# Norms of a segment made together, ahead of the first stacks, and the second weight group fetched behind x

## The chip, the cores and the metric

The kernel runs on one core of a Trainium2 chip. The core has TensorE (PE in the profile; PEld is its weight load) for matmuls, VectorE (DVE), ScalarE (ACT), GpSimd (POOL), and SyncE (SP), on whose queue this kernel issues its DMAs. Each engine works through its own list of instructions in order; semaphores make one engine wait for another. The metric is device time in microseconds (us), less is better.

## The reference

One block of a transformer whose layer norms are modulated by a condition vector c. First a memory-augmented causal attention over four segments of 512 tokens (32 heads of 32), then a mixer MLP across the tokens. Cut to what matters:

```python
mod = silu(c) @ w_mod                       # six rows of 1024: sa, ca, ga, sb, cb, gb
h = layernorm(x) * (1 + ca) + sa            # x: 2048 x 1024, float32
q, k, v = h @ wq, h @ wk, h @ wv            # 32 heads
for s in range(4):                          # segments of 512 tokens
    p = softmax(q[s] @ k[s].T * scale + mask)
    o[s] = g * (phi(q[s]) @ M) / (phi(q[s]) @ z) + (1 - g) * (p @ v[s])
    M += phi(k[s]).T @ v[s];  z += phi(k[s]).sum()
x = x + ga * (o @ wo)
h = layernorm(x) * (1 + cb) + sb
x = x + gb * (w2.T @ gelu(w1.T @ layernorm(h) + b1) + b2)     # over the tokens
```

Only the first two lines and the beginning of the third and fourth, the opening of the kernel, are touched by the change.

## The kernel before, in words

All large products keep close to float32 accuracy by splitting each operand into a rounded high part and the rest (`split`: a cast for the high part, a subtraction for the low part) and making three matmuls of the parts.

*First segment.* SP fetches, in this order: half of the weights for the scale row 1 + ca (`wms`), the four x tiles of segment 0 (128 tokens by 1024), the other half, then eight tiles `wm` for the shift sa, with the first group's attention weights (`rawv`, `rawq`) between them, then the four x tiles of segment 1. TensorE makes the scale row in two halves (`scale_row`, L273); VectorE copies each half out of PSUM (`scale_columns`, L279), and small matmuls (L281) turn it into columns. Meanwhile `norm_x` normalises each x tile by itself: statistics on VectorE (L130, L132), Ln and Exp on ScalarE (L133, L134), four small VectorE operations (L136 to L138, L218), and a pass over the tile on ScalarE (L219). Then come eight chunks of 128 channels: `h_chunk` transposes the four tiles' columns on TensorE (L224), ScalarE applies scale and shift (L226), and a split makes a page (a tile `h`, 128 channels by 512 tokens, high and low part; 16 buffers, so both segments' 8 pages have room). `first_chunk` multiplies each page with the weights as soon as it is there: keys and values (`nps`, L195) and queries (`qps`, L203). VectorE also makes one pass over a `wm` tile per chunk (L314) for the shift.

*Steps.* Attention then goes by steps t: t = 0 is weight group 0 (four heads) with segment 0, t = 1 the same group with segment 1, t = 2 and 3 are group 1 with segments 0 and 1, and so on. `project(t, piece)` has four pieces: two halves of keys and values with their copies out of PSUM (L380, L381, L386), then the transposes of the keys (`kps`, L395) with the queries, their split into `sg`, and the stacks of heads 0 to 2 (three small DMAs each, L356 to L358, `sk` from `sg`), then the stack of head 3 and the memory update (L445). For t = 0 the matmuls are `first_chunk`'s. The maxima (L463), scores (L499 and following) and values (L528) of a head come in the loop behind.

*Weights.* Six float32 tiles of a group are made by `split_part` from three raw fetches (`raw`: 3 buffers), into `w`, which has 8 buffers. `keep_w` writes the six to DRAM (`wsp`, L176) so that the second pass over the groups reads them back. Before the change the second group is fetched by `load_w(1, 0)` from the loop, behind the last stack of step 0 on SP's queue.

*Order.* The program text gives every instruction a priority, earlier text first; `tc.high_priority()` puts a block ahead. The order of each engine's list is then worked out when the kernel is built, by a planner that runs the program against a modelled clock (`schedule_with_timeline_sim=True`) and takes, on each engine, the ready instruction of highest priority. `tc.issue_after(i)` ties what is traced in its block to come behind instruction i, on the engine of i only. So a change of one place can move the order elsewhere.

Of the kernel before, what the change touches and what calls it, by code (L numbers as in the profile page):

```python
# [7 lines left out]
F32 = mybir.dt.float32  # L8
# [3 lines left out]
AF = mybir.ActivationFunctionType  # L12
ALU = mybir.AluOpType
# [5 lines left out]
P = 128  # L19
# [6 lines left out]
EPS = 1e-5  # L26
# [18 lines left out]
def attention_and_mlp(ctx, tc, x, wq, wkv, wo, beta, w1, b1, w2, b2, c, wm_a, wm_b, out):  # L45
    nc = tc.nc
    V, A, G, T, SY = nc.vector, nc.scalar, nc.gpsimd, nc.tensor, nc.sync
# [13 lines left out]
    const = ctx.enter_context(tc.tile_pool(name="const", bufs=1))  # L61
# [3 lines left out]
    a = par.__enter__()  # L65
    scb, gaw = (a.tile([P, D], F32, name=n) for n in ("scb", "gaw"))
    acst_pool = tc.tile_pool(name="acst", bufs=1)
    acst = acst_pool.__enter__()
# [6 lines left out]
    def bank(tag, bufs, name):  # L75
        return psum.tile([P, 512], F32, tag=tag, bufs=bufs, name=name)

    A.preload_act_table_set("natural_log_exp_and_others")
    ident = top.tile([P, P], F32, name="ident")
# [14 lines left out]
    eps = const.tile([P, 1], F32, name="eps")  # L94
# [17 lines left out]
    saca = acst.tile([P, NK, 2], F32, name="saca")  # L112
# [5 lines left out]
    def split(dst, src, hi_eng, lo_eng):  # L118

        hi, lo = dst[:, 0], dst[:, 1]  # L120
        if hi_eng is A:
            last_hi[0] = A.copy(hi, src)  # L122
        else:
            hi_eng.tensor_copy(hi, src)
        lo_eng.tensor_tensor(lo, src, hi.bitcast(F32), op=ALU.subtract)  # L125

    def ln_stats(pool, src, tag):
        st = const.tile([P, 2, 6], F32, tag="st", bufs=4, name="st")
        for i in range(2):
            V.bn_stats(st[:, i], src[:, 512 * i:512 * i + 512])  # L130
        mv = const.tile([P, 4], F32, tag="mv", bufs=4, name="mv")
        V.bn_aggr(mv[:, 0:2], st)  # L132
        A.activation(mv[:, 2:3], mv[:, 1:2], AF.Ln, bias=eps)  # L133
        A.activation(mv[:, 2:3], mv[:, 2:3], AF.Exp, scale=-0.5)  # L134
        v, r0, t = mv[:, 1:2], mv[:, 2:3], mv[:, 3:4]
        V.tensor_scalar(t, v, EPS, r0, op0=ALU.add, op1=ALU.mult)  # L136
        V.tensor_scalar(t, t, -0.5, r0, op0=ALU.mult, op1=ALU.mult)
        V.tensor_scalar(r0, t, 1.5, r0, op0=ALU.add, op1=ALU.mult)  # L138
        return mv
# [4 lines left out]
    def new_page(name):  # L144
        return page.tile([P, 2, 512], F32R, tag="page", bufs=16, name=name)
# [5 lines left out]
    def fetch_part(g, kind, part):  # L151
        r = a.tile([P, D], F32, tag="raw", bufs=3, name=f"raw{kind}{g}_{part}")
        SY.dma_start(r, (wkv if kind == "v" else wq)[g, :, 1024 * part:1024 * part + 1024])
        return r

    def split_part(g, kind, part, r):

        for i in range(2):
            w = aw.tile([P, 2, 512], F32R, tag="w", bufs=8, name=f"w{kind}0_{g}_{part}_{i}")
            split(w, r[:, 512 * i:512 * i + 512], A, V)  # L160
            W[0, g][kind, 2 * part + i] = w
# [11 lines left out]
    def keep_w(g):  # L173
        for kind, n in (("v", 4), ("q", 2)):
            for i in range(n):
                SY.dma_start(wsp[g, i if kind == "v" else 4 + i], W[0, g][kind, i].bitcast(F32))  # L176
# [8 lines left out]
    W = {}  # L185
# [25 lines left out]
        SY.dma_start(t, x[P * tt:P * tt + P])  # L211
        return t

    last_norm = [None]

    def norm_x(pool, t):
        mv = ln_stats(pool, t, "a")
        last_norm[0] = V.tensor_scalar(mv[:, 3:4], mv[:, 0:1], -1.0, mv[:, 2:3], op0=ALU.mult, op1=ALU.mult)  # L218
        A.activation(t, t, AF.Identity, scale=mv[:, 2:3], bias=mv[:, 3:4])  # L219

    def h_chunk(pool, xs, seg, ct):
        ps = bank(*(("s1", 2), ("s2", 2))[ct % 2] if seg else ("s2", 2), f"hps{seg}_{ct}")
        for i in range(4):
            T.transpose(ps[:, 128 * i:128 * i + 128], xs[i][:, P * ct:P * ct + P], ident)  # L224
        h32 = pool.tile([P, L], F32, tag="h32", bufs=HB, name=f"h32_{seg}_{ct}")
        A.activation(h32, ps, AF.Identity, scale=saca[:, ct, 1:2], bias=saca[:, ct, 0:1])  # L226
        pg = new_page(f"h{seg}_{ct}")
        split(pg, h32, V if seg else A, V if ct % 2 or not seg else G)
        hpages[seg, ct] = pg

    def token_tile(tt):

# [21 lines left out]
    s2p = right.__enter__()  # L254
    left = tc.tile_pool(name="st1", bufs=1)
    s1p = left.__enter__()
# [9 lines left out]
    bc = s1p.tile([P, NK, P], F32, name="bc")  # L266
    rows = MZ.rearrange("p g n -> p (g n)")[0:1]

    def scale_row(cb):
        ps = bank(*(("ms", 1), ("s1", 2))[cb], f"srow{cb}")  # L270
        with tc.high_priority():
            for k in range(NK):
                mm = T.matmul(ps[0:1], sc[:, k:k + 1], scale_wm[4 * cb + k // 2][:, k % 2], start=(k == 0),  # L273
                              stop=(k == NK - 1))
        return ps, mm

    def scale_columns(cb, ps):
        with tc.issue_after(last_norm[0].ins):
            V.tensor_copy(rows[:, 512 * cb:512 * cb + 512], ps[0:1])  # L279
        for ct in range(4 * cb, 4 * cb + 4):  # L280
            T.matmul(scale_ps[:, ct:ct + 1], rows[:, P * ct:P * ct + P], ident[0:1, 0:1], start=True, stop=True,  # L281
                     skip_group_check=True)
        V.tensor_scalar_add(saca[:, 4 * cb:4 * cb + 4, 1], scale_ps[:, 4 * cb:4 * cb + 4], 1.0)

    fetch_scale(0)
    xs = {0: [load_x(s1p, tt) for tt in range(4)]}
# [8 lines left out]
        q_chunk(W[0, 0], h, ct, first[2])  # L295

    srow = [scale_row(0)]
    with tc.high_priority():
        for t in xs[0]:
            norm_x(s1p, t)  # L300
    srow.append(scale_row(1))
    V.tensor_copy(bc, sc.unsqueeze(2).to_broadcast([P, NK, P]))
    for i in range(2):
        ps = bank("s2", 2, f"scps{i}")
        with tc.issue_after(srow[0][1].ins):
            for j in range(4):
                T.transpose(ps[:, 128 * j:128 * j + 128], bc[:, 4 * i + j], ident)
        A.copy(scb[:, 512 * i:512 * i + 512], ps)
    for cb in range(2):
        scale_columns(cb, srow[cb][0])  # L310
    for ct in range(NK):
# [14 lines left out]
    b = late.__enter__()  # L326
# [19 lines left out]
    st = {}  # L346

    last_sk = {}
# [232 lines left out]
    seg_x = {}  # L581

    def seg_load(seg):
        seg_x[seg] = [load_x(s2p, tt) for tt in range(4 * seg, 4 * seg + 4)]
        for t in seg_x[seg]:
            norm_x(s2p, t)

    def seg_chunks(seg, lo, hi):
        for ct in range(lo, hi):
            h_chunk(s2p, seg_x[seg], seg, ct)  # L590

    def spread(dst, i):
        SY.dma_start(dst, bass.AP(tensor=modd.tensor, offset=modd.offset + D * i, ap=[[0, P], [1, D]]))

    project(0, 0)
    project(0, 1)
    with tc.issue_after(last_wm.ins):
        seg_load(1)
    project(0, 2)
    project(0, 3)  # L600
    seg_chunks(1, 0, 8)
    project(1, 0)
    project(1, 1)
    project(1, 2)
    project(1, 3)
    with tc.issue_after(last_sk[0, 3].ins):
        keep_w(0)
    right.__exit__(None, None, None)
    right = tc.tile_pool(name="late2", bufs=1, side="right", reuse_waits="tile")
    r_ = right.__enter__()  # L610
# [47 lines left out]
    for n in range(-LEADS, 4 * NI + VL):  # L658
# [3 lines left out]
        m = n + LEADP  # L662
        if 0 <= m + 4 < 4 * NI:
            t = (m + 4) // 4
# [5 lines left out]
        if 59 <= m < 67:  # L670
            seg, ct = 2 + (m - 59) // 4, 2 * ((m - 59) % 4)
            reload_h(seg, ct)
            reload_h(seg, ct + 1)
        if 4 * NI - 5 <= m < 4 * NI + 3:
            i = m - 4 * NI + 5
# [434 lines left out]
```

## Time and profile before

| what | value |
|---|---|
| median of 3 runs | 2245.69 us (2245.46 to 2247.83) |
| the profiled execution's own time | 2248.87 us |
| its span | 2247.2 us |
| TensorE busy, share of the span | 2196.9 us, 98% |
| VectorE, ScalarE, GpSimd busy | 1670.9, 1144.3, 725.4 us |
| DMA, mean over the span | 188 GB/s |

A row of the timeline reads: start, time, engine, line, operation, output<-input, shape, count, and in brackets how long the engine had been idle before and what ended that. Rows of the same kind are merged, so a row can span a pause; matmul ends are modelled. A row of a table of stretches gives the busy time of each engine in a stretch. A row of the waits gives who waited for whom, the total, how many times, and the longest. The chain that ended last is the path back from the last instruction through whatever released each step.

### The profile page before, as it was taken

The numbers are of one execution on the slowest core, as the hardware profiler recorded it, in microseconds if no ns is written. First come the engines' busy times: TensorE is split into PE (matmuls) and PEld (weight loads), VectorE is DVE, ScalarE is ACT, GpSimd is POOL, SyncE is SP. The second block draws the span as 40 slices with busy tenths as digits, with TensorE's granted clock in tenths as the row PEclk, the third lists the DMA queues.
The fourth block names the chain that finished last, engine by engine and source line by source line (L and its number), as shares of the span: only waits on it lengthen the run. The fifth ranks groups of instructions, "written<-read, shape, count | busy, mean of one in ns | idle before, by whom it ended". The sixth has DMA issues, their size and how long they took to land.

```text
span 2247.2 us, 38334 instructions
## 1 busy us (share of the span) xinstructions
PE 2196.9 (98%) x13786; PEld 1890.3 (84%) x13786; DVE 1670.9 (74%) x3782; ACT 1144.3 (51%) x2098; POOL 725.4 (32%) x831
## 2 busy tenths in 40 slices
PE   8999999998999999999999999999999999999999
PEld 5889898887988899988888888888888888888887
DVE  6677677766677677665758866788888887868687
ACT  5477777665666666655546633533334242424232
POOL 1166666655766677655001200033330000000000
PEclk9999999999999999999999999999999999999999
DMA  7656565687567566674664587755556541414134
GB/s 267 199 169 186 162 190 165 181 290 228 145 188 223 164 185 196 192 215 161 225 217 154 215 323 272 262 188 221 206 202 239 204 155 57 155 57 145 57 122 150
DMA packets 175187, 423.06 MB, mean 188 GB/s; under 512 B 17525, under 2 KB 71829, under 8 KB 166037
## 3 DMA queue, kind: packets, MB, share of 16 engines
q1 hardware_dynamic: 174996, 420.61, 57.3%
q8 instruction: 110, 1.80, 0.3%
q14 instruction: 81, 0.66, 0.1%
HBM read 244.62 MB, written 125.06 MB: 165 GB/s over the span
## 4 chain that ended last, share of the span: by engine, by line
PE 85%; DMA 5%; DVE 4%; ACT 2%; POOL 2%; issue 1%; SPq 1%; DVEq 0%; ACTq 0%; POOLq 0%
PE mx L890 47%; PE nps L195 12%; PE qps L203 7%; PE po L760 6%; PE pv L528 3%; DMA sk<-sg 1%; PE sz L463 1%; PE a L499 1%; PE sx L463 1%; PE a L502 1%; PE sy L463 1%; POOL ph L514 1%; PE rd L435 1%; DMA sk<-nt 1%; PE up L445 1%
## 5 line engine op out<-in xcount | busy, mean ns | idle before, releaser
L890 PE MATMUL mx<-bU,sp 128*128 128x512 f32 x2352 | 534.2, 389 | 0.9 <-DVE ac L897 0.9
L890 PEld LDWEIGHTS mx<-bU,sp 128*128 128x128 f32 x2352 | 441.2, 188 | 93.4 <-issue 1.3
L195 PE MATMUL nps<-wv,h 128*128 128x256 f32 x3072 | 436.2, 282 | 0.0
L122 ACT CAST sp<-wr 128x384 fp32r<-128x384 f32 (+2 forms) x408 | 217.1, 545 | 425.0 <-PE mx L890 357.6
L890 PE MATMUL mx<-bA,sp 128*128 128x512 f32 x1764 | 430.5, 389 | 0.0
L514 POOL TENSOR_TENSOR ph<-p,ph 128x640 f16<-128x640 f32 x256 | 377.5, 1496 | 150.1 <-ACT ph L512 148.3
L195 PEld LDWEIGHTS nps<-wv,h 128*128 128x128 f32 x3072 | 405.0, 189 | 6.2
L890 PEld LDWEIGHTS mx<-bA,sp 128*128 128x128 f32 x1764 | 331.1, 188 | 68.8
L125 DVE TENSOR_TENSOR sp<-wr,sp 128x384 fp32r<-128x384 f32 (+2 forms) x408 | 259.4, 646 | 28.3 <-ACT sp L122 28.1
L897 DVE TENSOR_TENSOR ac<-mx,ac 128x512 f32<-128x512 f32 x280 | 189.1, 684 | 84.7 <-PE mx L890 84.1
L203 PE MATMUL qps<-h,wq 128*128 128x512 f32 x768 | 200.4, 404 | 0.0
L512 ACT CAST ph<-p 128x1280 f16<-128x1280 f32 x128 | 161.0, 1259 | 45.8 <-POOL p L510 45.2
L760 PE MATMUL po<-wo,ots 128*128 128x512 f32 x768 | 179.3, 390 | 0.0
L760 PEld LDWEIGHTS po<-wo,ots 128*128 128x128 f32 x768 | 143.5, 188 | 29.0
L203 PEld LDWEIGHTS qps<-h,wq 128*128 128x128 f32 x768 | 143.4, 193 | 28.0
L510 POOL TENSOR_SCALAR_AFFINE_SELECT p<-p 128x256 f32<-128x256 f32 x256 | 129.0, 513 | 109.1 <-ACT p L507 61.3
L890 PE MATMUL mx<-bB,sp 128*128 128x512 f32 x588 | 164.0, 389 | 0.0
L528 PE MATMUL pv<-vp,ph 128*128 128x97 bf16 (+1 forms) x2560 | 144.4, 203 | 2.4 <-POOL ph L514 1.6
L465 DVE CUSTOM_DVE_ANT_0 sx<-sx,mask 128x128 f32<-128x128 f32 (+1 forms) x256 | 93.7, 366 | 60.6 <-PE sx L463 58.5
L528 PEld LDWEIGHTS <-ph 128*128 128x128 f16 x2560 | 115.6, 99 | 24.9 <-issue 10.0
L890 PEld LDWEIGHTS mx<-bB,sp 128*128 128x128 f32 x588 | 110.3, 188 | 22.9
L897 DVE TENSOR_TENSOR cc<-mx,cc 128x512 f32<-128x512 f32 x140 | 94.7, 683 | 36.5 <-PE mx L890 36.4
(199 smaller groups left out, 3158.2 us busy)
## 6 DMA issues: line engine op xcount, KB each, us to landing
sk<-sg SPq DMA_DIRECT2D x384, 128.0 KB
wr<-in_w_dram SPq DMA_DIRECT2D x28, 1024.0 KB
wr<-in_w_dram SPq DMA_DIRECT2D x32, 768.0 KB
bstu<-ucd SPq DMA_DIRECT2D x28, 768.0 KB
wsp<-wv SPq DMA_DIRECT2D x32, 512.0 KB
rawm<-in_wm_b_dram SPq DMA_DIRECT2D x32, 512.0 KB
wv<-wsp SPq DMA_DIRECT2D x32, 512.0 KB
pcd<-cc SPq DMA_DIRECT2D x14, 1024.0 KB
```

The lines of the kernel that those rows point to most:

```text
L122: last_hi[0] = A.copy(hi, src)
L125: lo_eng.tensor_tensor(lo, src, hi.bitcast(F32), op=ALU.subtract)
L195: T.matmul(ps[:, aa], h[:, j, 128 * tt:128 * tt + 128], wt[:, i, o:o + 256], start=(n == 0), stop=(n >= 6 * NK - 2), skip_group_check=True)
L203: T.matmul(ps, wt[:, i, o:o + 128], h[:, j], start=(k + n == 0), stop=(3 * k + n == 3 * NK - 1))
L465: marks[4 * t + h - LEADS, "V"] = V.tensor_tensor_reduce(o, o, mask[:, 384 - 128 * i:], 1.0, -3.0e38, op0=ALU.add, op1=ALU.max, accum_out= ...
L510: G.affine_select(w, w, pattern=[[0, 2], [1, 128]], compare_op=ALU.is_ge, fill=0.0, base=0, channel_multiplier=-1)
L512: marks[n, "A"] = A.copy(ph[:, 0], p32)
L514: marks[n, "G"] = G.tensor_tensor(ph[:, 1, c], p32[:, c], ph[:, 0, c], op=ALU.subtract)
L528: T.matmul(pv[:, i, 0:w], ph[:, part, o:o + 128], d["vp"][:, j, h, 0:w], start=(n == 0), stop=(n == 19), skip_group_check=True)
L760: T.matmul(ps, os_[:, i, P * ct:P * ct + P], wop[ct, nh][:, j], start=(n == 0), stop=(n == 3 * NK - 1))
L890: T.matmul(ps, ops[q][:, i, P * k:P * k + P], b[:, j], start=(m == 0 and first), stop=(m == 3 * nk - 1), skip_group_check=True)
L897: V.tensor_tensor(d, ps, d, op=ALU.add)
```

## The change

- `norm_all` takes four tiles. VectorE makes all statistics into one tile `mv4`; one Ln and one Exp on 128x4, four small VectorE operations on 128x4 (now `scalar_tensor_tensor`), then the passes over the tiles: the first and third on ScalarE (`activation`), the second and fourth on VectorE (`tensor_scalar`). All of it has high priority. It returns marks: the last statistics, the Exp, and the last pass of either engine. `norm_x` stays for the tiles of segments 2 and 3.
- First segment: the transposes of sc and their copies (L307, L308) stand ahead of the norms and lose their tie to the first scale row. The copies of the scale rows are tied to the last statistics instead of the last norm.
- Second segment: `seg_load(1)` stands ahead of `project(0, 0)`. ScalarE's part of pieces 0 and 1 is tied behind its Exp; VectorE's part of everything down to piece 3 behind its last tile pass. The pages 0 and 1 of segment 1 come next, and pieces 2 and 3 of step 0, with the stacks, are tied behind ScalarE's and VectorE's work for page 1. The other six pages follow.
- Weights: the three raw fetches of group 1 are issued right behind x of segment 1; the splits are tied behind page 1 on both engines; `keep_w(1)` is tied behind the last stack of step 0, as `keep_w(0)` is. The loop finds group 1 present and does not load it.

No arithmetic of the result is left out.

```diff
--- before.py
+++ after.py
@@ -122,7 +122,7 @@
             last_hi[0] = A.copy(hi, src)
         else:
             hi_eng.tensor_copy(hi, src)
-        lo_eng.tensor_tensor(lo, src, hi.bitcast(F32), op=ALU.subtract)
+        return lo_eng.tensor_tensor(lo, src, hi.bitcast(F32), op=ALU.subtract)
 
     def ln_stats(pool, src, tag):
         st = const.tile([P, 2, 6], F32, tag="st", bufs=4, name="st")
@@ -211,11 +211,33 @@
         SY.dma_start(t, x[P * tt:P * tt + P])
         return t
 
-    last_norm = [None]
+    def norm_all(tiles):
+
+        with tc.high_priority():
+            m = acst.tile([P, 5, 4], F32, tag="mv4", bufs=1, name="mv4")
+            r, t, nb = m[:, 2], m[:, 3], m[:, 4]
+            mv = m[:, 0:2].rearrange("p a b -> p (a b)").rearrange("p (i a) -> p i a", a=2)
+            for k, src in enumerate(tiles):
+                st = const.tile([P, 2, 6], F32, tag="st", bufs=4, name="st")
+                for i in range(2):
+                    V.bn_stats(st[:, i], src[:, 512 * i:512 * i + 512])
+                last_stats = V.bn_aggr(mv[:, k], st)
+            A.activation(r, mv[:, :, 1], AF.Ln, bias=eps)
+            exp = A.activation(r, r, AF.Exp, scale=-0.5)
+            V.scalar_tensor_tensor(t, mv[:, :, 1], EPS, r, op0=ALU.add, op1=ALU.mult)
+            V.scalar_tensor_tensor(t, t, -0.5, r, op0=ALU.mult, op1=ALU.mult)
+            V.scalar_tensor_tensor(r, t, 1.5, r, op0=ALU.add, op1=ALU.mult)
+            V.scalar_tensor_tensor(nb, mv[:, :, 0], -1.0, r, op0=ALU.mult, op1=ALU.mult)
+            for k, src in enumerate(tiles):
+                if k % 2:
+                    last_v = V.tensor_scalar(src, src, r[:, k:k + 1], nb[:, k:k + 1], op0=ALU.mult, op1=ALU.add)
+                else:
+                    last_a = A.activation(src, src, AF.Identity, scale=r[:, k:k + 1], bias=nb[:, k:k + 1])
+        return last_stats, exp, last_a, last_v
 
     def norm_x(pool, t):
         mv = ln_stats(pool, t, "a")
-        last_norm[0] = V.tensor_scalar(mv[:, 3:4], mv[:, 0:1], -1.0, mv[:, 2:3], op0=ALU.mult, op1=ALU.mult)
+        V.tensor_scalar(mv[:, 3:4], mv[:, 0:1], -1.0, mv[:, 2:3], op0=ALU.mult, op1=ALU.mult)
         A.activation(t, t, AF.Identity, scale=mv[:, 2:3], bias=mv[:, 3:4])
 
     def h_chunk(pool, xs, seg, ct):
@@ -223,10 +245,11 @@
         for i in range(4):
             T.transpose(ps[:, 128 * i:128 * i + 128], xs[i][:, P * ct:P * ct + P], ident)
         h32 = pool.tile([P, L], F32, tag="h32", bufs=HB, name=f"h32_{seg}_{ct}")
-        A.activation(h32, ps, AF.Identity, scale=saca[:, ct, 1:2], bias=saca[:, ct, 0:1])
+        act = A.activation(h32, ps, AF.Identity, scale=saca[:, ct, 1:2], bias=saca[:, ct, 0:1])
         pg = new_page(f"h{seg}_{ct}")
-        split(pg, h32, V if seg else A, V if ct % 2 or not seg else G)
+        lo = split(pg, h32, V if seg else A, V if ct % 2 or not seg else G)
         hpages[seg, ct] = pg
+        return act, lo
 
     def token_tile(tt):
 
@@ -275,7 +298,7 @@
         return ps, mm
 
     def scale_columns(cb, ps):
-        with tc.issue_after(last_norm[0].ins):
+        with tc.issue_after(last_stats.ins):
             V.tensor_copy(rows[:, 512 * cb:512 * cb + 512], ps[0:1])
         for ct in range(4 * cb, 4 * cb + 4):
             T.matmul(scale_ps[:, ct:ct + 1], rows[:, P * ct:P * ct + P], ident[0:1, 0:1], start=True, stop=True,
@@ -295,17 +318,14 @@
         q_chunk(W[0, 0], h, ct, first[2])
 
     srow = [scale_row(0)]
-    with tc.high_priority():
-        for t in xs[0]:
-            norm_x(s1p, t)
-    srow.append(scale_row(1))
     V.tensor_copy(bc, sc.unsqueeze(2).to_broadcast([P, NK, P]))
     for i in range(2):
         ps = bank("s2", 2, f"scps{i}")
-        with tc.issue_after(srow[0][1].ins):
-            for j in range(4):
-                T.transpose(ps[:, 128 * j:128 * j + 128], bc[:, 4 * i + j], ident)
+        for j in range(4):
+            T.transpose(ps[:, 128 * j:128 * j + 128], bc[:, 4 * i + j], ident)
         A.copy(scb[:, 512 * i:512 * i + 512], ps)
+    last_stats = norm_all(xs[0])[0]
+    srow.append(scale_row(1))
     for cb in range(2):
         scale_columns(cb, srow[cb][0])
     for ct in range(NK):
@@ -582,29 +602,41 @@
 
     def seg_load(seg):
         seg_x[seg] = [load_x(s2p, tt) for tt in range(4 * seg, 4 * seg + 4)]
-        for t in seg_x[seg]:
-            norm_x(s2p, t)
+        return norm_all(seg_x[seg])
 
     def seg_chunks(seg, lo, hi):
         for ct in range(lo, hi):
-            h_chunk(s2p, seg_x[seg], seg, ct)
+            marks_ = h_chunk(s2p, seg_x[seg], seg, ct)
+        return marks_
 
     def spread(dst, i):
         SY.dma_start(dst, bass.AP(tensor=modd.tensor, offset=modd.offset + D * i, ap=[[0, P], [1, D]]))
 
-    project(0, 0)
-    project(0, 1)
     with tc.issue_after(last_wm.ins):
-        seg_load(1)
-    project(0, 2)
-    project(0, 3)
-    seg_chunks(1, 0, 8)
+        _, exp, _, normed_v = seg_load(1)
+    with tc.issue_after(normed_v.ins):
+        with tc.issue_after(exp.ins):
+            project(0, 0)
+            project(0, 1)
+        h_a, h_v = seg_chunks(1, 0, 2)
+        with tc.issue_after(h_a.ins), tc.issue_after(h_v.ins):
+            project(0, 2)
+            project(0, 3)
+    parts = (("v", 0), ("v", 1), ("q", 0))
+    raw_1 = [fetch_part(1, *part) for part in parts]
+    seg_chunks(1, 2, 8)
     project(1, 0)
     project(1, 1)
     project(1, 2)
     project(1, 3)
     with tc.issue_after(last_sk[0, 3].ins):
         keep_w(0)
+    W[0, 1] = {}
+    with tc.issue_after(h_a.ins), tc.issue_after(h_v.ins):
+        for part, r in zip(parts, raw_1):
+            split_part(1, *part, r)
+    with tc.issue_after(last_sk[0, 3].ins):
+        keep_w(1)
     right.__exit__(None, None, None)
     right = tc.tile_pool(name="late2", bufs=1, side="right", reuse_waits="tile")
     r_ = right.__enter__()
```

## The prediction

> **What bounds the kernel now.** I read the page first, then the stages of the opening in a table of stretches, then that stage instruction by instruction in the timeline. From the page come the span, TensorE's load and the engines' shares of the chain that ended last:
>
> ```profile
> span 2247.2 us, 38334 instructions
> PE 2196.9 (98%) x13786; PEld 1890.3 (84%) x13786; DVE 1670.9 (74%) x3782; ACT 1144.3 (51%) x2098; POOL 725.4 (32%) x831
> PE 85%; DMA 5%; DVE 4%; ACT 2%; POOL 2%; issue 1%; SPq 1%; DVEq 0%; ACTq 0%; POOLq 0%
> ```
>
> TensorE carries 85% of that chain. A change to the opening is therefore worth the time by which it lets TensorE go on sooner, as far as what follows does not wait for something else. The stretches show where TensorE stands still (length, then the busy time of TensorE, its weight load, VectorE, ScalarE and GpSimd with their instructions, granted clock, DMA share, GB/s):
>
> ```profile
> 27.00:47.00 20.00, 20.00 (x140) 18.78 (x139) 19.93 (x43) 12.22 (x21) 4.31 (x12) 0.93 0.58 230
> 47.00:60.00 13.00, 7.70 (x41) 6.07 (x41) 6.15 (x21) 11.43 (x24) 0.59 (x2) 0.74 0.50 106
> 60.00:100.00 40.00, 36.71 (x278) 34.38 (x277) 27.95 (x71) 16.91 (x36) 5.58 (x6) 1.00 0.77 256
> ```
>
> Between 47 and 60 TensorE is busy for 7.70 of 13 us, at a granted clock of 0.74, while ScalarE is busy for 11.43: this is where the second segment is normalised. Before it, from 27 to 47, both TensorE (20.00) and VectorE (19.93) are full. The timeline of the first segment's norms:
>
> ```profile
> 12.28 0.21 DVE L132 BATCH_NORM_AGGREGATE mv<-st 128x2 f32<-128x12 f32 x1
> 13.56 0.20 DVE L136 TENSOR_SCALAR mv<-mv 128x1 f32<-128x1 f32 x1
> 14.62 1.09 PE L307 MATMUL scps<-ident,bc 128*128 128x128 f32 x8
> 16.10 7.03 PE L273 MATMUL srow<-wms,sc 128*1 128x512 f32 x16 [0.39 <-DMA wms<-in_wm_a_dram]
> 17.66 0.20 DVE L132 BATCH_NORM_AGGREGATE mv<-st 128x2 f32<-128x12 f32 x1
> 18.99 2.36 ACT L219 ACTIVATE x<-x,mv 128x1024 f32<-128x1024 f32 x2
> 21.48 0.21 DVE L136 TENSOR_SCALAR mv<-mv 128x1 f32<-128x1 f32 x1 [2.79 <-ACT mv L134]
> 22.35 0.67 DVE L279 COPY MZ<-srow 1x512 f32<-1x512 f32 x1
> 22.47 1.24 ACT L219 ACTIVATE x<-x,mv 128x1024 f32<-128x1024 f32 x1 [1.03 <-DVE mv L218]
> 22.95 1.20 DVE L314 SCALAR_TENSOR_TENSOR wm<-wm,scb 128x1024 f32<-128x1024 f32 x1
> 25.53 0.78 ACT L226 ACTIVATE h<-hps,saca 128x512 f32<-128x512 f32 x1 [0.79 <-DVE saca L283]
> 26.34 0.62 ACT L122 CAST h<-h 128x512 fp32r<-128x512 f32 x1
> 27.23 1.20 PE L195 MATMUL nps<-wv,h 128*128 128x256 f32 x4
> ```
>
> The last tile's statistics are there at 17.86, but its small operations start at 21.48: ScalarE put two 1.2 us tile passes ahead of its Exp, and VectorE stood for 2.79 us. The copy of the scale row (L279), tied to the last norm, waits until 22.35. The first projection matmul comes at 27.23. And for the second segment:
>
> ```profile
> 40.08 1.26 DVE L130 BATCH_NORM_STATS2 st<-x 128x6 f32<-128x512 f32 x2
> 46.29 0.26 DVE L132 BATCH_NORM_AGGREGATE mv<-st 128x2 f32<-128x12 f32 x2
> 50.52 1.30 ACT L219 ACTIVATE x<-x,mv 128x1024 f32<-128x1024 f32 x1
> 54.27 3.51 ACT L219 ACTIVATE x<-x,mv 128x1024 f32<-128x1024 f32 x3 [1.15 <-DVE mv L218]
> 58.20 2.12 ACT L226 ACTIVATE h<-hps,saca 128x512 f32<-128x512 f32 x3 [0.42 <-PE hps L224]
> 59.01 0.43 DVE L124 CAST h<-h 128x512 fp32r<-128x512 f32 x1 [2.25 <-ACT h L226]
> 59.50 0.73 PE L195 MATMUL nps<-wv,h 128*128 128x256 f32 x4
> 68.68 0.69 DVE L125 TENSOR_TENSOR h<-h,h 128x512 fp32r<-128x512 f32 x1
> ```
>
> Statistics end at 46.55, yet the last tile is normalised only at 57.78, 11.2 us later, because the copies and stacks of the first step (t = 0) sit between. TensorE begins the projection of t = 1 at 59.50; the last of its eight pages is finished at 69.37. Then the second group's weights:
>
> ```profile
> 50.70 0.73 SPq L356 DMA_DIRECT2D sk<-sg  x1
> 59.79 3.32 SPq L176 DMA_DIRECT2D wsp<-wv  x4
> 65.68 2.48 SPq L153 DMA_DIRECT2D rawv<-in_wkv_dram  x2
> 64.39 8.05 PE L195 MATMUL nps<-wv,h 128*128 128x256 f32 x68
> 72.89 2.41 ACT L122 CAST wv<-rawv 128x512 fp32r<-128x512 f32 x4 [1.75 <-DMA rawv<-in_wkv_dram]
> 75.20 0.36 ACT L380 COPY k<-nps 128x256 f32<-128x256 f32 x1
> 76.17 5.77 PE L203 MATMUL qps<-h,wq 128*128 128x512 f32 x24
> ```
>
> Their fetch (L153) is issued at 65.68, behind twelve stack transfers and six write-backs of the first group's weights (L176). ScalarE waits 1.75 us for it, then makes four splits, and only then, at 75.20, copies the second half of t = 1's keys, although the matmuls for it ended at 72.44. TensorE's next long piece, the queries, starts at 76.17.
>
> **The change part by part.** *First segment.* Four Ln/Exp pairs and four sets of four small VectorE operations become one pair and one set on 128x4. By the rows, statistics to first small operation is 13.56 - 12.49 = 1.07 us, and a set is 22.47 - 21.48 = 0.99. So the factors stand at 17.86 + 1.07 + 0.99 = 19.9. ScalarE's two tiles (2 x 1.24) end at 22.4 instead of 23.71. VectorE's two have no row in this form: a 128x512 f32 cast takes 0.43, so a 128x1024 pass is at least about 0.86, and at most the 1.20 of the L314 pass. I take 0.86, the nearer form with one tensor read, 1.7 for both; at 2.4 they still end by 22.3, before ScalarE's. Not on the path. TensorE could not use it before 23.13 anyway, when the second scale row's matmuls end (16.10 + 7.03). What remains is the row copy, freed from 22.35 to about 17.9, and with it the scale columns: 23.13, some 0.6 for four transposes (half of the 1.09 for the eight of L307), the h activation at 0.78 and its rounding at 0.62 give 25.1, and with the handovers 25.5 instead of 27.23 for the first projection: 1.7 sooner (bounds: 0, if the columns still come behind both rows, and 2.1). VectorE loses 12 small operations of 0.2 (2.4 us) and gains two tiles (1.7): nothing either way. The transposes of sc and their copies move ahead of the norms; they lie now in the pause before 16.10, where TensorE ends up waiting for a DMA (the 0.39 in the row), and cost 1.09 where no such pause covers them.
>
> *Second segment.* Its statistics now have priority, and the copies of t = 0 go behind its Exp on ScalarE and behind its last VectorE tile. When does x arrive? The rate of the DMA over the first 60 us, in 40 slices of 1.5 us:
>
> ```profile
> GB/s 0 32 178 423 426 415 418 410 415 404 407 418 404 404 415 410 415 407 404 418 404 407 396 404 415 202 16 0 0 0 0 0 5 0 60 190 193 172 94 205
> ```
>
> The stream stops in slice 26, near 38.5 us, so at 512 KB a tile and 410 GB/s (1.28 us each) the four land from about 34.7 to 38.5. VectorE is full then, and whatever order the planner chooses, its work up to the last statistic is the same; it only starts sooner, by up to the 1.7 above, of which I count 1.1. That puts the last statistic at 45.4 instead of 46.55. In the worst case the statistics go ahead of the last first-segment pages (eight at 0.63 and four sums at 0.2, 5.9 us), TensorE starves for 2 to 3 us near 43, but the norm is earlier by the same amount, so the two orders cost alike. From 45.4: 1.07, 0.99 and 2.5 on ScalarE give tiles normalised at 49.9 instead of 57.78, and by the old distance (59.50 - 57.78 = 1.7) TensorE starts t = 1 at 51.6, 7.9 us sooner.
>
> Not all of it stays. Of ScalarE's 11.43 us in the stretch 47 to 60, 4.8 were norm passes and 1.8 page activations; the other 4.8 belong mostly to t = 0. Its six copies of k and v (0.36 each by the row at 75.20) can fill the wait for the small operations; two stack roundings, two exponential passes, one rounding of v and the first two weight splits, seven passes at about 0.62, 4.3 us, now lie among the eight page activations. ScalarE waited there:
>
> ```profile
> ACT h L226 <- POOL h L125: 2.5, 3, 1.0
> ```
>
> Those 2.5 us absorb part, so pages take 1.6 to 4 us longer than the old 11.2 (58.20 to 69.37); I take 2.8, the middle. The first page begins 1.3 us before the matmuls (58.20 to 59.50), so at 50.3, and the last is done at 50.3 + 11.2 + 2.8 = 64.3 instead of 69.37, a gain of 5.1 (3.9 to 6.3).
>
> *Weights.* Three 512 KB fetches move past twelve stacks and six write-backs in SP's queue to right behind x. Their three raw buffers are free by then, and nothing stands behind them on SP until the stacks. At the 410 GB/s of the slices they take 3.8 us and land near 43, in a stretch where the DMA did nothing. The old wait goes: the copy at 75.20 could have run at 72.44, 2.8 us. What is late next is room: eight weight buffers, six held by the first group until t = 1 has used them and they are written back. The stacks start behind page 1, I reckon 54.6 instead of 50.70; write-backs then start at 63.7 instead of 59.79 and have read the first four tiles by about 68, while t = 1's matmuls end near 67.3 (64.3 + 3.0). I charge 0.7 of the 2.8 (ends: 0 and all of it), gain 2.1. Behind a late split on ScalarE stand the key copy and the transposes that TensorE needs.
>
> Later stacks cost nothing while TensorE has the projections of t = 1 and t = 2 (36.71 busy of 40 in 60 to 100); if that cover is gone, the 3.9 us are paid in full.
>
> *Sum.* 5.1 + 2.1 = 7.2 us at the queries of t = 1 (bounds 3.9 and 9.1). The profiled execution took 2248.87 us, its span and 1.67 around it; minus 7.2 is 2241.7. It stands 3.18 above the median of the runs, 2245.69, so I forecast 2238.5.
>
> *The clock.* After the pause the granted clock was half for at least this piece:
>
> ```profile
> 54.00:56.40 2.40, 2.14 (x10) 2.17 (x11) 0.98 (x8) 2.12 (x2) 0.00 (x0) 0.50 0.95 203
> ```
>
> [...]
>
> **Rivals.** *Larger gain.* The order falls well: pages do not slow (6.3 or more instead of 5.1), no new wait for buffers (2.8), and the first projection's 1.7 us survives: 6.3 + 2.8 + 1.7 = 10.8, 2234.9. For it: VectorE's 2.79 us pause is real. Against: ScalarE must hold all moved work.
>
> *The write-back becomes the new wait.* If the planner sets all six splits ahead of the key copy and the first group is still being written, the 2.8 us stays and another 0.8 is lost: 7.2 - 2.1 - 0.8 = 4.3, 2241.4. For it: buffers for two tiles only. Against: in the old order these writes were done in time.
>
> *Hidden anyway.* The attention loop behind it is not all TensorE. These rows of its chain and of its waits are stack transfers:
>
> ```profile
> 519.54 11.22 DMA sk<-sg
> 559.63 7.12 DMA sk<-sg
> PE sx L463 <- DMA sk<-sg: 10.1, 2, 9.0
> ```
>
> A gain of 7 us can be given back before such a transfer, whose start depends on other transfers: 2245.7.
>
> *Slower.* The order of every queue is worked out anew when the opening changes. In the loop SP's queue carries page reloads, weights and stacks together; if a stack falls behind a batch of reloads once more for each of these two places, TensorE waits 11.2 + 7.1 = 18.3 us again: 2238.5 + 18.3 = 2256.8. It decides from 7.2 us of such waits, and shows as slower by 0.2% from 11.7. For it: two such waits exist. Against: the order of the plan's due steps in the loop is untouched.
>
> **How the numbers follow.** About 0.2% (4.5 us) is what a measurement of this kernel can tell from no change. Forecast 0.45 (own range 2236 to 2241), larger gain 0.15, write-back 0.10, hidden 0.10, slower 0.20. So faster 0.60, same 0.20, slower 0.20. The range runs from the larger gain less 6 us of the loop's own waits, which may fall away as well (one is 7.12), 2229, up into the slower case, 2251; some 0.05 lies below and 0.12 above.
>
> **What would show it.** Right: the first projection before 26.5; the second segment's four norm passes shared by two engines and ended by about 50; t = 1's first matmul near 51.6; L153 of the second group issued by 33 and no wait of ScalarE for its data; the queries of t = 1 near 69. Wrong: h32 activations of the second segment spread over more than 15 us; ScalarE or VectorE waiting at a weight split for a write-back; or the loop's waits for stack transfers growing by more than 7 us while the opening did shrink.

## The result, and the profile after

| | median | ratio to before, 95% interval |
|---|---|---|
| before, 8 runs | 2246.22 us (2245.37 to 2247.83) | |
| changed, 8 runs | 2239.40 us (2238.21 to 2240.15) | 0.9969 (0.9958 to 0.9979) |

The change makes the kernel 6.8 us faster (by the interval 4.7 to 9.4); 2238.5 was forecast. The profiled execution took 2239.78 us, against 2248.87 before; the latter lies some 3 us above its median. First the stretches of the opening, in the columns of the prediction's table:

```profile
27.00:47.00 20.00, 19.24 (x139) 17.22 (x137) 19.52 (x39) 11.47 (x19) 4.30 (x12) 1.00 0.74 300
47.00:60.00 13.00, 9.30 (x66) 7.36 (x64) 10.18 (x18) 11.14 (x22) 2.70 (x2) 1.00 0.30 69
60.00:100.00 40.00, 39.18 (x274) 35.77 (x275) 27.07 (x75) 15.07 (x33) 3.35 (x5) 1.00 0.68 229
```

From 27 to 47 little is changed. Between 47 and 60 TensorE is busy for 9.30 us instead of 7.70, at full clock instead of 0.74 (two further executions of the same program had 0.87 there, see f2 and g3), and in the 40 us behind it for 39.18 instead of 36.71. The timeline of the first segment:

```profile
16.33 0.66 DVE L302 COPY MZ<-srow 1x512 f32<-1x512 f32 x1
17.87 2.37 ACT L235 ACTIVATE x<-x,mv 128x1024 f32<-128x1024 f32 x2 [0.82 <-DVE mv L230]
17.87 1.53 DVE L233 TENSOR_SCALAR x<-x,mv 128x1024 f32<-128x1024 f32 x2
18.89 5.31 PE L296 MATMUL srow<-wms,sc 128*1 128x512 f32 x12
20.70 1.23 DVE L334 SCALAR_TENSOR_TENSOR wm<-wm,scb 128x1024 f32<-128x1024 f32 x1 [1.23 <-DMA wm<-in_wm_a_dram]
24.24 0.68 DVE L302 COPY MZ<-srow 1x512 f32<-1x512 f32 x1 [2.31 <-PE srow L296]
26.55 0.72 PE L195 MATMUL nps<-wv,h 128*128 128x256 f32 x4
```

The norms end at 20.24 on ScalarE and 19.40 on VectorE, 3.5 us sooner than 23.71. But VectorE then stands 1.23 us for the first `wm` tile and 2.31 us for the second scale row, and the first projection comes only 0.68 us sooner (26.55, before 27.23). TensorE ends that second row at 24.20, before at 23.13: the transposes of sc and the columns of the first row now stand ahead of its last matmuls. The second segment, its stacks and the weights:

```profile
29.50 1.55 SPq L153 DMA_DIRECT2D rawv<-in_wkv_dram  x2
46.20 0.32 DVE L224 BATCH_NORM_AGGREGATE mv<-st 128x2 f32<-128x12 f32 x3
47.72 0.16 DVE L230 SCALAR_TENSOR_TENSOR mv<-mv 128x4 f32<-128x4 f32 x1
47.91 1.53 DVE L233 TENSOR_SCALAR x<-x,mv 128x1024 f32<-128x1024 f32 x2
48.58 2.41 ACT L235 ACTIVATE x<-x,mv 128x1024 f32<-128x1024 f32 x2
51.52 1.45 ACT L248 ACTIVATE h<-hps,saca 128x512 f32<-128x512 f32 x2 [0.53 <-PE hps L246]
52.81 0.51 PE L195 MATMUL nps<-wv,h 128*128 128x256 f32 x2
53.00 1.41 DVE L124 CAST h<-h 128x512 fp32r<-128x512 f32 x1 [0.24 <-ACT h L248]
53.96 1.39 SPq L376 DMA_DIRECT2D sk<-sg  x2
62.21 3.20 SPq L176 DMA_DIRECT2D wsp<-wv  x4
65.42 0.62 ACT L122 CAST wv<-rawv 128x512 fp32r<-128x512 f32 x1 [1.66 <-DMA wsp<-wv]
65.97 0.68 DVE L125 TENSOR_TENSOR h<-h,h 128x512 fp32r<-128x512 f32 x1
69.94 0.38 ACT L400 COPY k<-nps 128x256 f32<-128x256 f32 x1 [0.43 <-PE nps L195]
70.92 5.87 PE L203 MATMUL qps<-h,wq 128*128 128x512 f32 x24
```

The last statistic ends at 46.52, as before (46.55). The four tiles are normalised at 50.99 instead of 57.78, t = 1 starts at 52.81 instead of 59.50, the last page ends at 66.65 instead of 69.37, and the queries of t = 1 start at 70.92 instead of 76.17. ScalarE now waits 1.66 us for the first group's write-back (`wsp` from `wv`), but t = 1's matmuls are still running then: the key copy comes at 69.94, as soon as they end. So the opening gives 5.25 us at the queries.

Behind that the loop brings differences of its own. The waits of TensorE between 100 and 1100 us:

```profile
PE sx L463 <- DMA sk<-sg: 10.4, 3, 9.0
```

```profile
PE sx L483 <- DMA sk<-sg: 6.9, 3, 5.3
```

Before stands first, the changed kernel second: 10.4 us for stack transfers against 6.9.

### The profile page after: what moved, and what is told of

Its sections match the earlier page's. It is cut to its first block, busy times and chain, and to the rows that moved or that the text cites. A ratio compares the mean times of both kernels' runs of the same rounds, so it can differ in the third digit from the quotient of the medians.

```text
span 2238.1 us, 38277 instructions
## 1 busy us (share of the span) xinstructions
PE 2199.5 (98%) x13786; PEld 1888.4 (84%) x13786; DVE 1679.5 (75%) x3762; ACT 1137.1 (51%) x2082; POOL 731.0 (33%) x831
## 4 chain that ended last, share of the span: by engine, by line
PE 85%; DMA 4%; POOL 3%; DVE 3%; ACT 3%; issue 2%; SPq 1%; ACTq 0%; DVEq 0%; POOLq 0%
PE mx L922 48%; PE nps L195 10%; PE po L792 8%; PE qps L203 7%; PE pv L548 3%; POOL ph L534 2%; PE a L519 1%; PE sz L483 1%; PE sx L483 1%; DMA sk<-sg 1%; ACT ph L532 1%; PE a L522 1%; DVE wv L125 1%; DMA sk<-nt 1%; PE srow L296 1%
## 5 line engine op out<-in xcount | busy, mean ns | idle before, releaser
L195 PE MATMUL nps<-wv,h 128*128 128x256 f32 x3072 | 441.7, 283 | 1.2 <-DVE h L125 0.5
L534 POOL TENSOR_TENSOR ph<-p,ph 128x640 f16<-128x640 f32 x256 | 382.3, 1514 | 157.1 <-ACT ph L532 154.2
L530 POOL TENSOR_SCALAR_AFFINE_SELECT p<-p 128x256 f32<-128x256 f32 x256 | 123.5, 493 | 99.7 <-ACT p L527 51.6
```

Of the source, the lines that this page charges most:

```text
L195: T.matmul(ps[:, aa], h[:, j, 128 * tt:128 * tt + 128], wt[:, i, o:o + 256], start=(n == 0), stop=(n >= 6 * NK - 2), skip_group_check=True)
L530: G.affine_select(w, w, pattern=[[0, 2], [1, 128]], compare_op=ALU.is_ge, fill=0.0, base=0, channel_multiplier=-1)
L534: marks[n, "G"] = G.tensor_tensor(ph[:, 1, c], p32[:, c], ph[:, 0, c], op=ALU.subtract)
```

## The experiments

All ratios are to the kernel before in the same job; the runs of before spread from 2241.9 to 2253.8 us over these jobs, so a difference under some 2 us is not read from the times. "Queries" is the start of t = 1's queries in the profile (before: 76.17).

The planner's order can be read apart from time. Taken from the traces, from entry 900 of TensorE's 13786 matmuls on (near 150 us) the kernels fall into families: before, e2 and e4 have one and the same order; the changed kernel, e1, f1, f2, f3, f4, g1, g2 and g3 another; e3 has a third. The first two part at entry 3665 (477 us before, 471 us in the changed kernel).

**e1, norms only.** The fetch from the loop as before; the lines of the weights part are removed:

```diff
-    raw_1 = [fetch_part(1, *part) for part in parts]
...
-    W[0, 1] = {}
...
-            split_part(1, *part, r)
...
-        keep_w(1)
```

> The changed kernel without its weights part: group 1 is fetched from the loop again, behind the stacks and write-backs. Theory (the two parts lie one behind the other on the path): the first matmul of t = 1 stays near 52.8 us, but the fetch is issued near 68 to 70, ScalarE waits for it, and the queries of t = 1 start between 74 and 78 instead of 70.92; time 2243 to 2247. Rival (norms alone carry the gain, the weights are hidden anyway): queries near 71, time 2238 to 2241.

Measured: 0.9974 (0.9963 to 0.9985), 2241.46 against 2246.92. Queries at 69.40. The theory, that the parts lie one behind the other, fell; the rival's reading of the trace held, its time (2238 to 2241) nearly. ScalarE and TensorE in the timeline of e1:

```profile
68.42 0.37 ACT L400 COPY k<-nps 128x256 f32<-128x256 f32 x1 [1.19 <-PE nps L195]
76.13 1.14 ACT L122 CAST wv<-rawv 128x512 fp32r<-128x512 f32 x2 [5.01 <-DMA rawv<-in_wkv_dram]
69.40 5.87 PE L203 MATMUL qps<-h,wq 128*128 128x512 f32 x24
76.80 3.80 PE L195 MATMUL nps<-wv,h 128*128 128x256 f32 x28 [1.06 <-ACT wv L122]
```

The wait for the fetch is longer than before, 5.01 us instead of 1.75, but the key copy (68.42) no longer stands behind it on ScalarE. It costs TensorE 1.06 us ahead of t = 2. And without splits among the pages the queries come 1.5 us sooner than in the changed kernel: at the queries the norms alone give 6.8 us, more than both parts together.

**e2, weights only.** The kernel before, with the fetch behind x and the splits tied behind page 1:

```diff
         seg_load(1)
+    raw_1 = [fetch_part(1, *part) for part in parts]
...
-    seg_chunks(1, 0, 8)
+    h_a, h_v = seg_chunks(1, 0, 2)
+    seg_chunks(1, 2, 8)
```

> The kernel before with only the early fetch and the splits behind page 1. Theory: first matmul of t = 1 stays near 59.5, the wait of 1.75 us goes, the key copy follows the last matmul at 72.4, queries of t = 1 start near 73.4 instead of 76.17; time 2242.5 to 2244.5. Rival (the fetch was hidden): queries near 76, 2246.

Measured: 0.9980 (0.9969 to 0.9991), 2243.35. First matmul of t = 1 at 59.64, queries at 74.70: 1.5 us sooner, where 2.8 was expected, since the last page now ends at 71.29 instead of 69.37. The wait for the fetch is gone; the splits take part of it back. So each part alone removes the wait before the key copy, and they do not add.

**e3, together but not ahead.**

```diff
-    with tc.issue_after(last_wm.ins):
-        _, exp, _, normed_v = seg_load(1)
-    with tc.issue_after(normed_v.ins):
-        with tc.issue_after(exp.ins):
-            project(0, 0)
-            project(0, 1)
-        h_a, h_v = seg_chunks(1, 0, 2)
-        with tc.issue_after(h_a.ins), tc.issue_after(h_v.ins):
-            project(0, 2)
-            project(0, 3)
+    project(0, 0)
+    project(0, 1)
+    with tc.issue_after(last_wm.ins):
+        seg_load(1)
...
+    project(0, 2)
+    project(0, 3)
+    h_a, h_v = seg_chunks(1, 0, 2)
```

> The changed kernel with the norms made together but the text order of before: pieces 0 and 1 of t = 0 ahead of the second segment's norms, pieces 2 and 3 ahead of the pages, no marks. Theory (the gain is in the order, norms ahead of the first stacks): the stack splits go ahead of the pages again, first matmul of t = 1 at 54 to 56, queries at 73 to 75, time 2241 to 2244. Rival (making the norms together is enough, since they have priority anyway): first matmul within 1 us of 52.8, time within 1.5 us of the changed kernel.

Measured: 0.9972 (0.9963 to 0.9982), 2240.52. First matmul of t = 1 at 57.46, queries at 72.71. The first matmul is later even than the theory's 54 to 56, the queries and the time are just under its ranges. What it says of the order holds: priority alone did not put the norms first. On ScalarE the Ln came behind the six copies of t = 0, and the Exp behind two stack roundings and an exponential pass of it. The timeline of e3:

```profile
47.81 0.35 ACT L225 ACTIVATE mv<-mv,eps 128x4 f32<-128x4 f32 x1
49.47 0.27 ACT L226 ACTIVATE mv<-mv 128x4 f32<-128x4 f32 x1
52.02 2.37 ACT L235 ACTIVATE x<-x,mv 128x1024 f32<-128x1024 f32 x2 [1.23 <-DVE mv L230]
57.46 0.72 PE L195 MATMUL nps<-wv,h 128*128 128x256 f32 x4
```

Being ahead is thus worth 4.65 us at the first matmul and 1.8 at the queries. The time does not show it: this kernel's loop has the third order, and it is as fast as the changed one, as the rival said.

**e4, first segment as before.** `norm_x` for each tile of segment 0, its old place and ties; the rest of the change kept.

```diff
-    last_stats = norm_all(xs[0])[0]
+    with tc.high_priority():
+        for t in xs[0]:
+            norm_x(s1p, t)
```

> The changed kernel with the first segment's norms and scale rows as before, the rest changed. Theory (TensorE's second scale row and VectorE's load bound the first chunks, not the norms): first projection near 27.2 instead of 26.55, the last statistic of the second segment within 0.5 us of 46.52, queries of t = 1 within 1 us of 70.92, time within 1 us of the changed kernel. Rival (the 1.7 us that were forecast for the first segment carry): everything 1 to 1.7 us later.

Measured: 0.9992 (0.9980 to 1.0004), 2244.36. First projection 27.87, last statistic 47.29, queries 71.95: 1.3, 0.8 and 1.0 us later than in the changed kernel, which by the numbers is nearer to the rival. But this execution was late before the edit could matter. The transposes of sc, which stand as they do before the change, start at 15.47, in the trace of before at 14.62:

```profile
15.47 1.09 PE L332 MATMUL scps<-ident,bc 128*128 128x128 f32 x8
```

Behind that it is as the theory says: from the last statistic to the queries it takes 24.66 us, in the changed kernel 24.40. The time is not: the queries are 4.2 us ahead of before, but only 1.8 us (by the interval -0.9 to 4.5) are left at the end, which neither theory has. In the chain of e4, at the entry to the output projection, stand two waits for a reload that the chain of before does not have there. The rows of e4 with the queries ahead of them and behind, then the same queries before:

```profile
877.85 4.43 PE qps L203 x19
925.09 4.43 DMA otr<-oT
934.06 4.97 DMA otr<-oT
966.36 2.10 PE qps L203 x9
```

```profile
886.61 4.36 PE qps L203 x19
970.85 2.07 PE qps L203 x9
```

So in these two executions a lead of 8.8 us shrinks to 4.5 there. One such wait each stands in the chains of e2 (4.32 us at 926.00) and of the changed kernel (4.13 at 924.64) too, and they keep their gain.

**f1, first segment only.** Second segment and weights as before.

```diff
-    with tc.issue_after(last_wm.ins):
-        _, exp, _, normed_v = seg_load(1)
+    project(0, 0)
+    project(0, 1)
+    with tc.issue_after(last_wm.ins):
+        seg_load(1)
...
-        return norm_all(seg_x[seg])
+        for t in seg_x[seg]:
+            norm_x(s2p, t)
```

> The kernel before with only the first segment's part of the change; second segment and weights as before. The planner gives it, from the second step group on, the same order of the loop as the changed kernel's, while the opening keeps its old waits. Theory of the shift (the gain is made in the opening and only carried): queries of t = 1 near 75.5 to 76, time 0 to 1 us under before. Rival (the other order of the loop gives part of it): queries the same 75.5 to 76, but the time 2.5 to 4 us under before, the stack waits near 520 us shorter.

Measured: 1.0006 (0.9995 to 1.0016), 2245.99 against 2245.77, queries at 76.24. This kernel has the changed kernel's order of the loop without its opening, and gains nothing: the theory of the shift holds, and the other order of the loop is not what made the kernel faster. The waits for stacks are indeed shorter in its trace, as the rival has it (TensorE at L483 4.9 us in all between 100 and 1100 us, before 10.4), but the time does not show it.

**f2, the changed kernel again.**

> The changed kernel once more, for comparison on one chip: queries of t = 1 near 70.9, 6 to 7.5 us under before by either theory.

Measured: 0.9970 (0.9959 to 0.9981), 2239.13, queries at 71.06. Against f1, with the same order behind, 5.2 us at the queries became 6.9 at the end. The stretches of the opening in f2 (the second is inside the first):

```profile
47.00:60.00 13.00, 10.25 (x66) 8.70 (x64) 10.10 (x18) 10.98 (x20) 2.67 (x2) 0.87 0.30 68
51.00:54.00 3.00, 2.98 (x14) 2.58 (x15) 1.36 (x2) 2.41 (x5) 1.10 (x1) 0.50 0.00 0
```

Here the clock was half from 51 to 54, and in g3 it was 0.55; in the profiled execution above it was 1.00.

**f3, late splits.** The weight splits tied behind the last page:

```diff
-    seg_chunks(1, 2, 8)
+    l_a, l_v = seg_chunks(1, 2, 8)
...
-    with tc.issue_after(h_a.ins), tc.issue_after(h_v.ins):
+    with tc.issue_after(l_a.ins), tc.issue_after(l_v.ins):
         for part, r in zip(parts, raw_1):
```

> The changed kernel with the weight splits tied behind the last page instead of page 1, same order of the loop. Theory (the splits among the pages cost 1.3 us): last page at 65.3 instead of 66.65, queries of t = 1 at 69.4 to 70 instead of 70.92, time 1 us under the changed kernel. Rival (the pages are bound by GpSimd's low parts, not by the splits): last page and queries as in the changed kernel, time within 0.5.

Measured: 0.9970 (0.9960 to 0.9980), 2239.49; last page at 64.99, queries at 69.38. The last statistic was already 0.37 us sooner in this execution (46.15), so the splits among the pages cost 1.3 us there, as the theory has it; the time, whose runs lie between 2235.77 and 2242.56, does not confirm that it reaches the end.

**f4 and g2, early write-back.** As f3, and the first group's write-back right behind the second group's fetch:

```diff
+    keep_w(0)
     l_a, l_v = seg_chunks(1, 2, 8)
...
-    with tc.issue_after(last_sk[0, 3].ins):
-        keep_w(0)
```

> As the one before, and the write-back of the first group is issued right behind the second group's fetch, where the DMA is idle, instead of behind the stacks. Theory (the wait for the write-back lies beside t = 1's matmuls): ScalarE's waits of 1.66 and 0.78 us for it go, queries within 0.5 us of the kernel with late splits, time the same within 1. Rival (the forecast's charge of 0.7 us and more for the write-back): 0.7 to 2.4 us less.

> The kernel with late splits and early write-back again, beside the changed kernel on one chip. If it is better, as the first time (2236.0 against 2239.1): 2 to 4 us under the changed kernel. If only the shift of the queries counts (69.5 against 71.0): 1.5 us under it.

Measured: f4 0.9962 (0.9950 to 0.9974), 2236.01 beside the changed kernel's 2239.13; g2, the same kernel in another job, 0.9952 (0.9937 to 0.9967), 2238.03 beside 2240.64. ScalarE has no wait for a write-back any more; queries at 69.48 and 69.13, as in f3. By the theory f4's time would be within 1 us of f3's, by the rival at most 2.4 under it; the medians are 3.5 apart, with intervals that overlap. The kernel is 2.6 to 3.1 us under the changed kernel both times, and 9.8 and 9.9 under before. The two intervals overlap with those of the changed kernel, so the difference between these two is likely, not shown.

**g1, low parts on VectorE.** As f4, without GpSimd in the second segment's pages:

```diff
-        lo = split(pg, h32, V if seg else A, V if ct % 2 or not seg else G)
+        lo = split(pg, h32, V if seg else A, V)
```

> The kernel with late splits and early write-back, and the low parts of the second segment's even pages on VectorE instead of GpSimd; same order of the loop as the changed kernel's. Theory (a GpSimd low part of 1.3 to 1.5 us holds up the VectorE instruction beside it by about 1 us, so four of them cost VectorE some 4 us and save it 4 x 0.69 = 2.8): no cast on VectorE near 1.4 to 1.6 us any more, last page 1 to 2 us sooner than 65.5, queries of t = 1 at 68 to 68.5, time 1 to 1.5 us under the kernel with early write-back. Rival (GpSimd's help is a gain): last page and queries 1 to 2 us later.

Measured: 0.9958 (0.9943 to 0.9973), 2238.21, level with g2. Last page at 63.29 instead of 65.16 (g2), 1.9 us sooner with one engine fewer, but queries at 68.79, only 0.3 sooner, and no 1 to 1.5 us in the time: from 53 to 69 TensorE is busy for 15.79 of 16 us, so its own work leaves no more room. The stretch in g1:

```profile
53.00:69.00 16.00, 15.79 (x131) 15.13 (x130) 14.16 (x31) 11.92 (x24) 0.11 (x1) 1.00 0.77 225
```

VectorE in the timelines, first the changed kernel's first cast with GpSimd's low part that follows it, then g1's:

```profile
52.33 0.43 DVE L124 CAST h<-h 128x512 fp32r<-128x512 f32 x1 [2.28 <-ACT h L248]
52.84 1.29 POOL L125 TENSOR_TENSOR h<-h,h 128x512 fp32r<-128x512 f32 x1 [6.11 <-DVE h L124]
```

```profile
53.06 0.69 DVE L125 TENSOR_TENSOR h<-h,h 128x512 fp32r<-128x512 f32 x1
53.67 0.42 DVE L124 CAST h<-h 128x512 fp32r<-128x512 f32 x1
```

With the row of 53.00 shown above (1.41), the cast took 0.43 alone and 1.41 while GpSimd subtracted. The cast that started at 53.00, 0.16 us behind the subtraction, ended at 54.41, 0.28 us behind the subtraction's end. In g1, without that subtraction, the two casts take 0.43 (52.60) and 0.42 (53.67). What the two engines contend for is not shown.

**g3, the changed kernel beside them.**

> The changed kernel beside the two: 6 to 7.5 us under before, queries of t = 1 near 71.

Measured: 0.9966 (0.9952 to 0.9980), 2240.64, queries at 70.70. Its profiled execution took 2243.3 us; that of f2, the same program on the same chip, 2236.6, with the queries 0.4 us later. So some 7 us of spread between single executions arise in the loop. The shorter of the two has the higher granted clock: its mean over the span is 0.997 in f2's trace and 0.993 in g3's. Over all runs taken beside f2 it is 0.992 on average for before, 0.994 for f1 and 0.995 for f2. Whether the clock makes the waits costly or the waits lower the clock, no run here separates.

## Why the prediction was right

The size and the place were right: the gain is made between the second segment's statistics and the queries of t = 1 (f1 against f2, with the same order behind), and most of it is carried. The way it was added up was not right, and that the median came within 1 us is in part luck. Point by point:

- *First segment, 1.7 us:* measured 0.68, inside the bounds (0 to 2.1). The norms were sooner than reckoned (20.24, forecast 22.4), since the statistics ended at 16.41, not 17.86, with no small operations between them. It helped no one: VectorE stood for the `wm` tile and for the second scale row. The forecast took that row to end at 23.13 as before; with the transposes of sc and the first columns ahead of it, it ended at 24.20. f1 (1.0006) shows that this part alone brings nothing.
- *Last statistic at 45.4:* wrong. It stayed at 46.52. The step that failed is "it only starts sooner": what VectorE gained at its start it lost to those two waits (1.23 and 2.31).
- *Normalised at 49.9, t = 1 at 51.6:* 50.99 and 52.81, late by that same 1.1. The distance from statistics to tiles was right (4.5 forecast, 4.47 measured), but by two errors that cancel: the factors stood at 47.88, 0.7 us sooner than reckoned from the statistic, and ScalarE was in the copies of t = 0 until 48.58. A VectorE tile pass was taken as 0.86; two took 1.53, so 0.77 each, below the lower end, which was an estimate from the 0.43 of a 128x512 cast; the `wm` pass, with two tensor inputs of 128x1024, took 1.23 in the same trace (20.70).
- *Pages 2.8 us longer:* 15.1 us from the first activation to the last low part against 11.2, so 4.0 longer, the upper end. f3 and e1 put 1.3 of it on the weight splits among the pages (18.8 us from the last statistic to the last page in both, 20.1 in the changed kernel). The rest goes with the work of t = 0, which no run takes away. The forecast counted ScalarE's passes for it, but from the first cast to the last low part VectorE was the fuller engine, 14.01 of 14.32 us against ScalarE's 9.29:

```profile
52.33:66.65 14.32, 12.54 (x100) 11.78 (x101) 14.01 (x24) 9.29 (x15) 5.47 (x5) 1.00 0.71 200
```

  What g1 saves (1.9 us) is no part of the 4.0, since before has the same four subtractions on GpSimd among its pages. The gain at the last page was 2.7, forecast 5.1 (3.9 to 6.3): this is the term that was mis-sized, by 1.2 for the late start and 1.1 for the longer pages.
- *Weights, 2.1 us:* the stretch from the last page to the queries shrank from 6.8 to 4.3 us, by 2.5. The forecast's new wait for the write-back is there (1.66 and 0.78 us); it was named as a sign of being wrong, but it costs nothing at the queries, since it lies beside matmuls (f4 and g2, without it, have them where f3 has). But the 2.5 are not the early fetch's: with the norms ahead, the planner put the key copy before the splits by itself. e1, without the weights part, has the queries at 69.40, 1.5 us sooner than the changed kernel. Beside the norms the weights part gave nothing at the queries, and its splits among the pages cost 1.3.
- *Sum, 7.2:* 5.25 at the queries, 6.8 at the end. The two terms do not add: alone, the norms give 6.8 at the queries (e1) and the weights 1.5 (e2), together 5.25. That the median was met although the queries fell 2 us short is luck: the loop behind them added 1.6 us. These 1.6 are within the interval of the result; the spread of the loop is larger, and its clock differs between the kernels (0.994 for f1, 0.995 for f2), so they are not given a cause.
- *The clock:* the sum takes nothing for it, and rightly. Before, the granted clock fell within TensorE's pause of 3.28 us that ends at 51.87: it was 0.69 from 50 to 51 and 0.50 from 51 to 57. The row that ends this pause, and the row that ends the longest pause of TensorE between 27 and 51 us in g3:

```profile
51.87 1.12 PE L224 MATMUL hps<-ident,x 128*128 128x128 f32 x4 [3.28 <-ACT x L219]
```

```profile
49.84 0.88 PE L246 MATMUL hps<-ident,x 128*128 128x128 f32 x6 [1.25 <-ACT x L235]
```

  In the profiled execution of the changed kernel the granted clock was 1.00 from 47 to 60, but f2 and g3, the same program, had 0.87. The longest pause ahead of the half clock of g3 was 1.25 us, as in the profiled execution (to 49.92), where no half clock followed; so the length of the pause does not tell these two apart. The full clock does not show at the queries: from the last statistic to them it is 24.40 us with it, and 24.68 (f2) and 24.26 (g3) without it.

The rivals: "hidden anyway" and "slower" did not come, as f2 and g3 repeat the gain; nor did the larger gain (2234.9). e4 shows that "hidden" was near: with an opening only 1.0 us later at the queries it kept 0.0008 of the 0.0031. The rival's place (stacks near 520 us) was not the one seen there. Why e4's reloads came late there, and why e2 kept more than its 1.5 us at the queries, is open: both have the order of before in the loop, so the order does not tell them apart, and no run here holds the transfers or the clock fixed.

## What to carry to other kernels

When an engine's list holds a long chain for the next stage (here four norms) and the copies of the last one, set the order by an explicit tie: e3 shows that a priority alone lost to whatever was ready first, by 4.65 us at the next matmul (though not in the time of this kernel). Reckon a freed engine's gain only up to its next input, and look for the same gain twice: two edits that each removed one wait did not add here (6.8 and 1.5 us alone, 5.25 together). Where a planner sorts everything behind an edit anew, compare the instruction lists first, and use a variant with the same list behind (f1) to tell a shift from luck.

## What the runs showed of the hardware that was not expected

- In the changed kernel's trace the four VectorE instructions that start 0.05 to 0.29 us behind a GpSimd subtraction of 128x512 float32 (1.29 to 1.42 us) take about 1 us longer than in g1: the casts at 53.00 and 64.17 take 1.41 and 1.53, in g1 0.42 to 0.43; the `scalar_tensor_tensor` at 58.73 takes 1.78 and the subtraction at 61.82 1.68, in g1 0.69 each. Four such subtractions given back to VectorE (0.69 each) made the pages end 1.9 us sooner (g1 against g2).
- ScalarE's Ln on 128x4 took 0.30 us in both segments of the changed kernel, on 128x1 0.28 to 0.35 before; the four small VectorE operations took 0.16 each on 128x4, 0.15 to 0.22 before on 128x1 (another instruction form). In these rows four columns took about the time of one.
- The same program on the same chip ended 6.7 us apart in two executions, though its openings agreed within 0.4 us; the mean granted clock was 0.997 in the shorter one and 0.993 in the longer.
- From 51 to 54 us the granted clock was 0.50 in f2, 0.55 in g3 and 1.00 in the profiled execution of the same program; the longest pause of TensorE between 27 and 51 us was 1.25 us in g3 and in the profiled execution alike.
